# A spectral filter with a gated feed-forward: more block products of seven, maxima over partitions by matmul, and a table of due times

## The chip, the cores and the metric

The kernel runs on one core of a Trainium2 chip. The metric is the device time of one execution in microseconds (us). The core has five engines, each of which works through its own instructions in program order: TensorE (PE), with its weight loads shown apart (PEld), VectorE (DVE), ScalarE (ACT), GpSimd (POOL) and SyncE (SP), which issues nearly all DMAs.

## The reference

x is 2048 rows by 512 columns, F is 1376; everything is f32.

```python
xn = _layernorm(x, axis=-1)
X = rfft2(xn, axes=(-2, -1)) * (w_r + 1j * w_i)
s = irfft2(X, s=(2048, 512), axes=(-2, -1))
gate = xn @ W_gate
gate = gate * (gate > 0)
h = gate * (xn @ W_up)
out = x + s * silu(h @ W_down)
```

## The kernel before, in words

Every product of matrices is made of f16 parts: each operand is split into a high part and a low part (high = round to f16, on ACT mostly; low = value less high, on DVE), and three passes, high x high, high x low, low x high, are added in PSUM (`PASSES`). A first few products of row block 0 use f32 operands, before the split ones are there (`whole` in `product`, L854).

**The feed-forward.** The 2048 rows are four row blocks c of 512 (`NBL` = 4). F is cut into eleven tiles f of 128 columns, the last (f = 10) of 96. For each c and f, `product` (L837) makes gate and up, [128 of F] x [512 rows], with 12 matmuls of 512 columns each; `rectify` (L883) takes the gate's positive part r on ACT, `hidden` (L895) multiplies it with up on DVE and splits the result into h. `down` (L916) adds the eleven tiles into four results dn of 128 rows x 512 columns for each block, and `gate` (L935) makes g = silu(dn) on ACT. The g of blocks 0 to 2 go to DRAM (G_d) and come back later, those of block 3 stay.

Ten of the eleven tiles form five pairs, `PAIRS` = (0,1), (3,4), (5,6), (7,8), (2,9). A pair has 2 x 2 tiles of 12 matmuls of 512 columns, 48 in all. `fast_products` (L944) makes the same 2 x 2 block product with seven block products of eight, from sums and differences of the blocks (D is halved, and the 512 rows are halved): seven times 12 matmuls of 256 columns, into three PSUM tiles sa, sb, sc, which ACT copies or rectifies on their way (sb from sa, sk from sc, sr and sq the positive parts) and DVE adds and multiplies (sc, se, sr). It needs two things ahead of it: `row_sums` (L478) of the row block, four sums sx of normalised rows, split, written to DRAM and brought back transposed as xS; and `weight_sums` (L682) of the pair, which loads the raw weights again (rp), scales them on ACT, makes four sums on DVE, and splits them into wT and into the place of part of up's weights in wgu. So after it the pair can't be made in the plain way.

Before, `PLAINS` says which pairs of which block are fast: in block 3 the pairs 0, 2, 3 and 4; all others are plain.

**The scales.** Weights are scaled by powers of two before they are split. The one for W_down needs the greatest value over all 128 partitions of a column md, the filter's needs that of mw. `greatest` (L728) writes the column to a row in DRAM and reads the row back onto all partitions, then takes the maximum on DVE. The scale scd and with it the split of W_down's rows (wds) wait for this.

**The filter.** The 2-D transform runs in stages of matmuls over eight chunks. Chunk c of x is folded and split (`fold`, `split`), the first stage (L582, tile s) goes to DRAM as A_d (from a tile t); for each of eight chunks q of the other axis, `fft_chunk` (L1026) has the stages y, xx, the filter (tt, pf), z and v, with a split (ACT the high half, DVE the low) between any two, and writes C_d; `last_stage` (L1188) reads ct from C_d, makes s2 on PE, and adds and subtracts halves on DVE and POOL (zz, ae, ye) into sv. `finish` (L1237) multiplies sv by g and adds x: for a chunk whose entry in `ADDS` is 'DMA', SP copies x to the output early and POOL issues an accumulating DMA of the product; else x is loaded into xt, added on DVE and stored by SP.

**What sets the order.** Every piece of work is a `step` (L123) of the class `Plan` with an engine, a cost, what it reads and writes, a due time and, for loads, a lead. `run` (L142) passes due times backwards from each step to those it needs, then fills the engines greedily: each time the step that can begin first, among those of one engine that can begin within 0.06 us the one with the smallest due. The steps are then written out in that order, so that the order on each engine is fixed. Tables at the top of the file (due times, which engine does which sum) are its inputs. All instructions are issued through one helper and so have one line in the profile, L87 (L197 after the change): tiles tell them apart.

## Time and profile before

| what | before |
|---|---|
| runs | 405.9, 404.8, 405.76 us |
| median | 405.76 us |
| profiled execution | 403.82 us |
| its span in the trace | 402.0 us |
| PE busy, matmuls | 394.6 us, 3148 |
| DVE busy | 324.1 us |
| ACT busy | 232.2 us |
| POOL busy | 31.8 us |

The span is from the first to the last thing that the profile records; the profiled execution has 1.82 us around it. In the listings below a row of a group reads: line, engine, operation, tile written <- tiles read (buffer numbers left out), shapes, count, then busy time in us, mean ns of one, and the idle time of the engine before them with what ended it. A row of the timeline begins with its start in us and its duration; what stands in brackets is the engine's idle time before it and what ended that. A row of waits reads: who waited <- for whom, us in total, times, longest. Busy time of a group counts overlapping instructions once.

### The profile page before, as it was taken

How to read it: one execution, taken by the hardware profiler on the slowest of the kernel's cores; microseconds unless marked ns; L12 is line 12 of the kernel's file. 1: busy time of each engine (PE TensorE's matmuls, PEld its weight loads, DVE VectorE, ACT ScalarE, POOL GpSimd, SP SyncE). 2: the span in 40 equal slices, each digit the busy share in tenths (PEclk: the TensorE clock that was granted, in tenths of full speed). 3: DMA queues.
4: the chain of work that ended last, by engine and by line, in shares of the span. 5: the costliest groups of instructions: out<-in, count | busy, mean ns of one | idle time of the engine just before them, and what ended most of it. 6: DMA issues, size and time to landing. Idle time of an engine off the chain costs nothing.

```text
span 402.0 us, 8180 instructions
## 1 busy us (share of the span) xinstructions
PE 394.6 (98%) x3148; PEld 225.4 (56%) x3148; DVE 324.1 (81%) x731; ACT 232.2 (58%) x458; POOL 31.8 (8%) x48
## 2 busy tenths in 40 slices
PE   8999998999999999999999999999999999999996
PEld 6954443544444454554545655556554766888545
DVE  4989997998978989369488589987995665988893
ACT  5999993578579954232563554736464635456311
POOL 0000000000000000014001020010110002404100
PEclk9999999999999999999999999999999999999999
DMA  7963220509599717924047009479445496967452
GB/s 253 398 222 104 91 55 7 157 11 228 180 307 322 247 51 298 230 98 127 31 122 247 2 1 292 142 237 228 104 90 178 139 237 212 197 193 182 110 182 105
DMA packets 53367, 66.50 MB, mean 165 GB/s; under 512 B 20752, under 2 KB 30832, under 8 KB 53328
## 3 DMA queue, kind: packets, MB, share of 16 engines
q1 hardware_dynamic: 52176, 63.89, 53.0%
q0 software_dynamic: 1152, 2.10, 3.4%
q8 instruction: 24, 0.39, 0.4%
q14 instruction: 15, 0.12, 0.1%
HBM read 42.89 MB, written 20.99 MB: 159 GB/s over the span
## 4 chain that ended last, share of the span: by engine, by line
PE 85%; ACT 9%; DMA 2%; DVE 1%; issue 1%; SPq 0%; ACTq 0%
PE gu L87 34%; PE dn L87 27%; PE sb L87 4%; ACT wgu L87 4%; PE s L87 3%; PE z L87 3%; PE sa L87 3%; PE xx L87 3%; PE sc L87 3%; DMA A_d<-t 2%; PE y L87 2%; PE small L87 2%; PE v L87 2%; ACT wds L87 1%; ACT r L87 1%; ACT xf L87 1%
## 5 line engine op out<-in xcount | busy, mean ns | idle before, releaser
L87 PE MATMUL gu<-xT,wgu 128*128 128x512 f16 (+1 forms) x768 | 165.3, 372 | 2.4 <-ACT r L87 1.8
L87 PEld LDWEIGHTS <-wgu 128*128 128x128 f16 x960 | 92.9, 98 | 89.3 <-issue 5.3
L87 PE MATMUL dn<-wds,h 128*128 128x512 f16 (+2 forms) x528 | 115.8, 372 | 0.3 <-ACT g L87 0.3
L87 PEld LDWEIGHTS <-h 128*128 128x128 f16 (+1 forms) x594 | 54.5, 98 | 56.2 <-issue 2.2
L87 ACT ACTIVATE h<-h 128x512 f16<-128x512 f32 (+1 forms) x36 | 22.0, 624 | 29.5 <-DVE h L87 29.5
L87 DVE TENSOR_TENSOR h<-gu,r 128x512 f32<-128x512 f32 (+3 forms) x44 | 27.6, 627 | 11.6 <-PE gu L87 8.6
L87 ACT ACTIVATE r<-gu 128x512 f32<-128x512 f32 (+2 forms) x36 | 20.7, 578 | 21.2 <-PE gu L87 18.2
L87 POOL TENSOR_TENSOR tt<-tt,tt 128x256 f32<-128x256 f32 x8 | 8.6, 1076 | 253.6 <-DVE tt L87 224.1
L87 DVE TENSOR_TENSOR h<-h,h 128x512 f16<-128x512 f32 (+1 forms) x36 | 23.8, 684 | 1.9 <-ACT h L87 1.8
L87 DVE SCALAR_TENSOR_TENSOR tt<-xsp,cw,wt 128x512 f32<-128x512 f32 x32 | 24.5, 819 | 0.0
L87 ACT ACTIVATE g<-dn,cdi 128x512 f32<-128x512 f32 (+1 forms) x16 | 10.8, 672 | 19.0 <-PE dn L87 17.4
L87 PE MATMUL gu<-xT,wgt 128*64 128x256 f16 (+1 forms) x144 | 17.0, 309 | 0.0
L87 DVE TENSOR_TENSOR z<-z,z 128x1024 f16<-128x1024 f32 x8 | 9.8, 1222 | 7.8 <-ACT z L87 7.7
L87 DVE TENSOR_TENSOR a<-y,a 128x1024 f16<-128x1024 f32 x8 | 9.7, 1223 | 7.9 <-ACT a L87 7.9
L87 PEld LDWEIGHTS <-wT 128*128 128x128 f16 x144 | 13.9, 98 | 3.1 <-issue 0.4
L87 DVE SCALAR_TENSOR_TENSOR wgu<-raw,p,wgu 128x512 f16<-128x512 f32 x20 | 14.5, 746 | 1.0 <-ACT wgu L87 1.0
L87 DVE TENSOR_TENSOR t<-v,t 128x1024 f16<-128x1024 f32 x8 | 9.7, 1220 | 6.8 <-ACT t L87 6.8
L87 ACT ACTIVATE z<-z 128x1024 f16<-128x1024 f32 x8 | 8.2, 1023 | 11.2 <-PE z L87 11.2
L87 DVE TENSOR_TENSOR t<-s,t 128x896 f16<-128x896 f32 (+1 forms) x16 | 10.6, 686 | 4.7 <-ACT t L87 4.7
L87 ACT ACTIVATE a<-y 128x1024 f16<-128x1024 f32 x8 | 8.1, 1024 | 9.5 <-PE y L87 9.5
L87 PEld LDWEIGHTS <-wgt 128*64 128x64 f16 (+1 forms) x144 | 9.7, 106 | 6.1 <-issue 0.8
L87 ACT ACTIVATE wgu<-raw 128x512 f16<-128x512 f32 x20 | 12.3, 620 | 0.0
(191 smaller groups left out, 596.8 us busy)
## 6 DMA issues: line engine op xcount, KB each, us to landing
A_d<-t SPq DMA_DIRECT2D x16, 256.0 KB, 4.1
rw<-in_wl SPq DMA_DIRECT2D x8, 512.0 KB, 5.9
wt<-in_wl SPq DMA_DIRECT2D x8, 512.0 KB, 7.0
at<-A_d SPq DMA_DIRECT2D x8, 512.0 KB, 5.2
C_d<-t SPq DMA_DIRECT2D x16, 256.0 KB, 3.4
ct<-C_d SPq DMA_DIRECT2D x16, 256.0 KB, 5.7
x<-in_x SPq DMA_DIRECT2D x7, 512.0 KB, 5.9
G_d<-g SPq DMA_DIRECT2D x12, 256.0 KB, 3.5
```

The source lines that it names most:

```text
L87: return lambda *args, **kw: self.tc.keep_in_program_order(f(*args, **kw))
```

## The change

1. `PLAINS` gives way to `fast(c, n)`, with `FASTS` = 2, 1, 2, 2, 2 blocks counted from the last. Block 3 then has all five pairs fast, block 2 the pairs 0, 2, 3 and 4: five more fast pairs in all. This adds `row_sums` for block 2 (with two more transposing DMAs) and `weight_sums` for pair 1, and the due times of the weight sums become a table (`TDUE`).
2. `weight_sums` keeps its raw weights in two tiles, one for gate and one for up, where it had one.
3. `greatest` multiplies a unit matrix by the column on DVE, brings it to all partitions with one f32 matmul by ones, and takes the maximum on DVE from PSUM. The two DMAs and the row in DRAM go.
4. After the backward pass of due times, `run` sets each step's due from a table `DUES`, and each lead from a table `WAITS`. With other numbers in the tables at the top (engines of some sums in `SUM2` and `DIFF2`, `ADDS` of chunk 5 now 'DMA', due times) this gives another order on every engine.

The counts: PE has 182 more matmuls (five times 84 less 48, and two), DVE 30 more rows in its list of instructions, ACT 20 more activations, POOL two more DMAs, SP two more transposes.

```diff
-STATS, ADDS, COPIES = ['DVE', 'DVE', 'ACT', 'DVE', 'ACT', 'ACT', 'ACT', 'ACT'], ['DMA', 'DMA', 'DVE', 'DMA', 'DMA', 'DVE', 'DVE', 'DVE'], [105.83, 259.66, 138.19, 267.03, 599.36, 405.66, 358.32, 606.44]
+STATS, ADDS, COPIES = ['DVE', 'DVE', 'ACT', 'DVE', 'ACT', 'ACT', 'ACT', 'ACT'], ['DMA', 'DMA', 'DVE', 'DMA', 'DMA', 'DMA', 'DVE', 'DVE'], [105.83, 202.31, 0.24, 342.73, 748.16, 416.58, 501.03, 895.66]
...
-TPREP, TSTEP, XLEAD = 205.365, 26.484, 13.97
+TDUE, XLEAD = [158, 242, 202, 219, 235], 17.37
...
-PLAINS = ['plain', 'plain', 'plain', 'plain', 'plain', 'plain', 'plain', 'plain', 'plain', 'plain', 'plain', 'plain', 'plain', 'plain', 'plain', 'fast', 'plain', 'fast', 'fast', 'fast']
+FASTS = ['2', '1', '2', '2', '2']
+DUES = (
+    61.11, 143.08, 138.41, 136.86, 1e+09, 1e+09, 1e+09, 1e+09, 1e+09, 1e+09, 1e+09, 1e+09, 1e+09, 1e+09, 1e+09, 1e+09, 1e+09, 1e+09, 1e+09, 1e+09,
...
+def fast(c, n):
+    return c >= NBL - int(FASTS[n])
...
+        for s, due in zip(steps, DUES):
+            s.due = due
+        for s, lead in zip([s for s in steps if s.lead is not None], WAITS):
+            s.lead = lead
...
-        tile_of(raw, "xg", [P, 2, 4, 2 * P], F32)
         for i, src in enumerate((wg, wu)):
+            tile_of(f"{raw}_{i}", "k4", [P, 4, 2 * P], F32)
...
-        row = dram.tile([1, P], F32, name=f"row_{name}")
-        tile_of(f"rows_{name}", "k2", [P, P], F32)
-        rows = lambda: T[f"rows_{name}"]
-        top = cpool.tile([P, 1], F32, name=f"max_{name}")
-        step("SP", .6, lambda: SP.dma_start(row.rearrange("a p -> p a"), col), reads=reads, writes=[f"row_{name}"], due=due, kb=8, lag=3.)
-        step("SP", .6, lambda: SP.dma_start(rows(), row.broadcast_to([P, P])), reads=[f"row_{name}"], writes=[f"rows_{name}"], kb=64, lag=5.2)
-        step("DVE", .22, lambda: DVE.tensor_reduce(top, rows(), axis=AX.X, op=ALU.max), reads=[f"rows_{name}"], writes=[f"all_{name}"], due=due + 10)
+        wide, top = f"wide_{name}", cpool.tile([P, 1], F32, name=f"max_{name}")
+        tile_of(wide, "k2", [P, P], F32)
+        tile_of(f"rows_{name}", "F", [P, P], F32)
+        step("DVE", .25, lambda: DVE.tensor_scalar(T[wide], unit, col, None, op0=ALU.mult), reads=reads, writes=[wide], port=True, due=due)
+        step("PE", .26, lambda: matmul(T[f"rows_{name}"], ones, T[wide], start=True, stop=True), reads=[wide], writes=[f"rows_{name}"], due=due + 2)
+        step("DVE", .3, lambda: DVE.tensor_reduce(top, T[f"rows_{name}"], axis=AX.X, op=ALU.max), reads=[f"rows_{name}"], writes=[f"all_{name}"], due=due + 4)
...
-        if c and f < TAIL and PLAINS[5 * c + n] == "fast":
+        if f < TAIL and fast(c, n):
...
-            if PLAINS[5 * c + n] == "plain":
+            if not fast(c, n):
...
-            if PLAINS[5 * c + n] == "fast" and PLAINS[5 * c - 5 + n] == "plain":
-                weight_sums(n, TPREP + n * TSTEP)
+            if c == NBL - int(FASTS[n]):
+                weight_sums(n, TDUE[n])
```

The order of the instructions is shown at two places. The first is SP's list from the start of the program, with the loads of x and of the raw weights of gate (in_wg) and up (in_wu). Before:

```order
1 L87 DMA x_143<-in_x 128x512 x2
2 L87 DMA raw_0_150<-in_wg 128x512
3 L87 DMA raw_1_155<-in_wu 128x512
4 L87 DMA x_170<-in_x 128x1024 [waits Pool_49]
5 L87 DMA raw_0_174<-in_wg 128x512 [waits Pool_49]
6 L87 DMA raw_1_187<-in_wu 128x512
7 L87 DMA raw_0_196<-in_wg 128x512
8 L87 DMA raw_1_203<-in_wu 128x512 [waits DMAHW0_49]
9 L87 DMA raw_0_212<-in_wg 128x1024 [waits DMAHW1_49]
10 L87 DMA raw_1_224<-in_wu 128x1024 [waits DMAHW2_49]
11 L87 DMA x_229<-in_x 128x1024 [waits DMAHW3_49]
12 L87 DMA x_240<-in_x 128x1024 [waits DMAHW4_49]
```

And after the change:

```order
1 L197 DMA x_141<-in_x 128x512 x2
2 L197 DMA raw_0_148<-in_wg 128x512
3 L197 DMA raw_1_153<-in_wu 128x512
4 L197 DMA x_157<-in_x 128x1024
5 L197 DMA x_161<-in_x 128x1024
6 L197 DMA x_177<-in_x 128x1024 [waits Pool_49]
7 L197 DMA raw_1_189<-in_wu 128x512
8 L197 DMA raw_0_182<-in_wg 128x512 [waits DMAHW0_49,Pool_49]
9 L197 DMA raw_1_208<-in_wu 128x1024 [waits DMAHW1_49]
10 L197 DMA raw_1_217<-in_wu 128x512 [waits DMAHW2_49]
11 L197 DMA raw_0_225<-in_wg 128x512 [waits DMAHW3_49]
12 L197 DMA raw_0_240<-in_wg 128x1024 [waits DMAHW4_49]
```

The x that waits for POOL is chunk 1, which with chunk 0 (row 1) makes row block 0. Chunks 2 and 3, rows 11 and 12 before, now stand ahead of it, as rows 4 and 5, and the weights behind it come in another order.

The second place is the end of DVE's list. sv_5252, sv_5353 and sv_5365 are the filter's results of chunks 7, 5 and 6; g_0 to g_3 are the gates dn3_0 to dn3_3 of row block 3, g_2l and g_3l those of block 2 that come back from DRAM. Before (sv_5044 and sv_5055 are chunks 6 and 7):

```order
674 L87 TENSOR_TENSOR sv_5044<-sv_5044,g_0_5006 128x512 [waits DVE_49,Activation_49]
675 L87 TENSOR_TENSOR sv_5044<-sv_5044,g_1_5072 128x512 [waits Activation_49]
676 L87 TENSOR_TENSOR xt_0_5051<-xt_0_5051,sv_5044 128x512 [waits DMAHW4_49,DVE_49]
677 L87 TENSOR_TENSOR sv_5055<-sv_5055,g_2_5123 128x512 [waits Activation_49]
678 L87 TENSOR_TENSOR xt_1_5065<-xt_1_5065,sv_5044 128x512 [waits DMAHW5_49,DVE_49]
679 L87 TENSOR_TENSOR xt_0_5086<-xt_0_5086,sv_5055 128x512 [waits DMAHW6_49,DVE_49]
680 L87 TENSOR_TENSOR sv_5055<-sv_5055,g_3_5191 128x256 [waits Activation_49]
681 L87 TENSOR_TENSOR xt_1_5092<-xt_1_5092,sv_5055 128x256 [waits DMAHW7_49,DVE_49]
682 L87 TENSOR_TENSOR sv_5055<-sv_5055,g_3_5191 128x128 [waits Activation_49]
```

After:

```order
702 L197 TENSOR_TENSOR sv_5252<-sv_5252,g_2_5389 128x512 [waits Activation_49]
703 L197 TENSOR_TENSOR sv_5353<-ye_5271 128x2x255
704 L197 TENSOR_TENSOR xt_0_5263<-xt_0_5263,sv_5252 128x512 [waits DMAHW5_49,DVE_49]
705 L197 TENSOR_TENSOR sv_5365<-sv_5365,g_1_5403 128x512 [waits Activation_49]
706 L197 TENSOR_TENSOR sv_5353<-sv_5353,g_2l 128x512 [waits DMAHW0_49,DVE_49]
707 L197 TENSOR_TENSOR sv_5252<-sv_5252,g_3_5439 128x128 [waits Activation_49]
708 L197 TENSOR_TENSOR sv_5353<-sv_5353,g_3l 128x512 [waits DMAHW1_49]
709 L197 TENSOR_TENSOR xt_1_5285<-xt_1_5285,sv_5252 128x128 [waits DMAHW7_49,DMAHW2_49,DVE_49]
710 L197 TENSOR_TENSOR xt_1_5371<-xt_1_5371,sv_5365 128x512 [waits DMAHW2_49]
...
715 L197 TENSOR_TENSOR xt_0_5408<-xt_0_5408,sv_5365 128x512 [waits DMAHW3_49]
```

Chunk 5 was finished before block 3's last gates, and its x was added on DVE. Now its second half (703) and its products by block 2's gates (706, 708) stand behind a product by g_2 of block 3 (702), POOL issues its two accumulating DMAs behind 706 and 708, and the list ends with the addition of x to chunk 6 (715).

More of the change, by code (lines that the diff above doesn't have):

```diff
@@ L706, in weight_sums @@
         minus((1, 0), (1, 1), (1, 0), U + [t1], t3)
-        minus((1, 1), (1, 1), (0, 0), U + [t1, t3], t2)
+        minus((1, 1), (1, 1), (0, 0), G + U + [t1, t3], t2)
         minus((0, 1), (0, 1), (1, 1), G + [t2], t4)
-        for to, of, needs, k in ((slice(0, 2), lambda: T[raw][:, 0].rearrange("p (t k) f -> p t k f", t=2), [t1, t4, t2], 0),
-                                 (slice(2, 3), lambda: B(1, 1).unsqueeze(1), [t2, t4], 2)):
+        for to, of, needs, k in ((slice(0, 2), lambda: T[f"{raw}_0"].rearrange("p (t k) f -> p t k f", t=2), [*G, t1, t4, t2], 0),
+                                 (slice(2, 3), lambda: B(1, 1).unsqueeze(1), [*U, t2, t4], 2)):
             m = 512 * (to.stop - to.start)
@@ L718, in weight_sums @@
             of = lambda j=j: B(1, 0)[:, :, j * P:j * P + P]
-            step("ACT", act(256), lambda to=to, of=of: ACT.activation(to(0), of(), AF.Copy), reads=[t3], writes=[("wgu", f, 0, 1)], due=due + 2)
-            step("DVE", dve(256), lambda to=to, of=of: DVE.tensor_sub(to(1), of(), to(0)), reads=[t3, ("wgu", f, 0, 1)], writes=[("wgu", f, 1, 1)], port=True, due=due + 4)
+            step("ACT", act(256), lambda to=to, of=of: ACT.activation(to(0), of(), AF.Copy), reads=[*U, t3], writes=[("wgu", f, 0, 1)], due=due + 2)
+            step("DVE", dve(256), lambda to=to, of=of: DVE.tensor_sub(to(1), of(), to(0)), reads=[*U, t3, ("wgu", f, 0, 1)], writes=[("wgu", f, 1, 1)], port=True, due=due + 4)
     def weights(f, i):
@@ L1293 @@
                 turn(k, LOWS[k])
-            if k > 1 and k % 2 and any("fast" in PLAINS[5 * (k // 2) + n] for n in range(len(PAIRS))):
+            if k > 1 and k % 2 and any(fast(k // 2, n) for n in range(len(PAIRS))):
                 row_sums(k // 2)
```

49 lines of the change are left out of this document (27 added, 22 removed), and 99 rows, old and new, of tables (DUES, WAITS).

## The prediction, on record before the run

> **What bounds the kernel now.** I read the page's busy times first, then TensorE's (PE's) waits, then the busy time of each engine in stretches of the span.
>
> ```profile
> span 402.0 us, 8180 instructions
> PE 394.6 (98%) x3148; PEld 225.4 (56%) x3148; DVE 324.1 (81%) x731; ACT 232.2 (58%) x458; POOL 31.8 (8%) x48
> PEclk9999999999999999999999999999999999999999
> GB/s 253 398 222 104 91 55 7 157 11 228 180 307 322 247 51 298 230 98 127 31 122 247 2 1 292 142 237 228 104 90 178 139 237 212 197 193 182 110 182 105
> ...
> PE gu L87 <- ACT r L87: 1.8, 1, 1.8
> PE small L87 <- DVE md L87: 1.1, 1, 1.1
> PE gu L87 <- DVE h L87: 0.6, 1, 0.6
> PE dn L87 <- ACT g L87: 0.3, 1, 0.3
> ```
>
> PE is busy 98% of the span at an undiminished clock, and its whole list of waits is 3.8 us, of which 1.1 us is the start. Removing PE columns therefore shows in the time, unless another engine becomes late. In the stretches (start:end, length, then busy time of PE, PEld, DVE, ACT, POOL) the same is seen:
>
> ```profile
> 97.00:176.00 79.00, 79.00 (x592) 38.75 (x591) 62.79 (x162) 47.75 (x90) 0.00 (x0) 1.00 0.71 229
> 176.00:283.00 107.00, 107.00 (x920) 57.87 (x919) 85.51 (x155) 54.55 (x84) 12.40 (x12) 1.00 0.48 140
> 283.00:362.00 79.00, 79.00 (x743) 51.64 (x742) 60.73 (x107) 39.71 (x77) 12.26 (x19) 1.00 0.65 167
> 362.00:402.00 40.00, 36.51 (x316) 24.36 (x313) 30.69 (x67) 12.30 (x34) 6.10 (x10) 1.00 0.53 145
> ```
>
> From 97 to 362 us PE stands still for nothing; VectorE (DVE) is busy 209.0 of those 265 us. DVE is the second bound: 56 us of room there, 21.5 us of it in the 107 us from 176 to 283.
>
> **Term 1, the products: -5.8 us.** A plain pair of gate and up is 48 matmuls of 512 columns. A fast pair is seven block products of 12 matmuls of 256 columns, 84 in all. The first row below is a run of 60 of the former, the next two are block products of block 3 that stand one behind the other; the last is the mean of one weight load.
>
> ```profile
> 23.95 13.11 PE L87 MATMUL gu<-xT,wgu 128*128 128x512 f16 x60
> ...
> 312.30 1.48 PE L87 MATMUL sa<-xT,wgu 128*128 128x256 f16 x12
> 313.62 1.47 PE L87 MATMUL sc<-xS,wgu 128*128 128x256 f16 x12
> ...
> L87 PE MATMUL gu<-xT,wgu 128*128 128x512 f16 x720 | 159.5, 379 | 1.8 <-ACT r L87 1.8
> L87 PE MATMUL gu<-xTf,raw 128*128 128x128 f32 x64 | 8.0, 278 | 0.1
> L87 PEld LDWEIGHTS <-wgu 128*128 128x128 f16 x960 | 92.9, 98 | 89.3 <-issue 5.3
> ```
>
> The 60 take 13.11 less the 0.38 of one alone over 59 steps, 0.216 us each, so a plain pair is 48 x 0.216 = 10.36 us. Twelve of the latter take 313.62 - 312.30 = 1.32 us, 0.110 each, so a fast pair is 7 x 1.32 = 9.2 us. The gain is 1.16 us a pair, and five pairs turn fast (four in block 2, pair 1 in block 3): -5.8 us. The down products keep their count and shape.
>
> A rule of the Trainium skill speaks against this term. Its page "TensorE: Matmul & The Clock Gate", section "Back-to-back issue gap", says that in a stream where each matmul has its own weight load the spacing is set by both, about 131 ns at 512 columns and 81 ns at 128; an estimate between them for 256 columns, about 98 ns, would make a fast pair 8.2 us against 6.3 us, a loss of 1.9 us a pair. The rows above give 216 and 110 ns, in step with the columns, so they do not agree, and the sum goes by the rows.
>
> **Term 2, maxima by matmul: +0.25 us on PE.** Two f32 matmuls of 128 columns are added; 64 such take 8.0 us, so 0.125 each. DVE's multiplication and maximum take the place of one maximum; below half a microsecond on DVE, in a stretch before 97 us and near 140 us. What this removes is in term 4.
>
> **Term 3, the head: +2.4 us (0 to 4.1).** In the new order two whole blocks of x (0.5 MB each) are issued ahead of the second half-block's x, on the same queue.
>
> ```profile
> 3.81 0.33 SPq L87 DMA_DIRECT2D x<-in_x  x1
> ...
> 17.61 1.58 PE L87 MATMUL gu<-xT,wgu 128*128 128x256 f16 x13
> ```
>
> This x, issued at 3.81, leads through statistics, normalisation and transposition to the first split products at 17.61. 1.05 MB more ahead of it take 2.6 us at the 398 GB/s of the second slice, 4.1 us at the 253 of the first, and nothing if PE's earlier work hides it. That work, f32 products on unsplit weights, is short of covering it, since its weights now come in another order too: I take 2.4, just under the faster rate.
>
> **Term 4, early waits: -2.7 us (0 to -2.7).** The way of the down weights' maximum through DRAM, before:
>
> ```profile
> 54.73 0.54 SPq L87 DMA_DIRECT2D row_md<-md  x1
> ...
> 64.14 0.32 SPq L87 DMA_DIRECT2D rows_md<-row_md  x1
> ...
> 65.00 0.63 ACT L87 ACTIVATE x<-xf 128x512 f16<-128x512 f32 x1 [5.03 <-DMA A_d<-t]
> ...
> 66.16 2.75 PE L87 MATMUL gu<-xT,wgu 128*128 128x512 f16 x12 [1.81 <-ACT r L87]
> ```
>
> The 128 writes of 4 bytes and the reading back occupy the queue from 54.73 past 64.14, while the memory moves 55 and then 7 GB/s. The transfers A_d<-t that stand beside them land late, ScalarE (ACT) waits 5.03 us for one, its r comes late, and PE waits 1.81 us. With the route through PE no DMA stands there. The 0.6 and 0.3 us of PE's list lie in the same setup (before 97 us), where a later start of PE gives ACT and DVE the time. I take all 2.7; none if ACT and DVE are as late as PE.
>
> **Term 5, more work on DVE and ACT: +0.9 us (0 to 15).** Mean durations on DVE:
>
> ```profile
> L87 DVE TENSOR_TENSOR h<-h,h 128x512 f16<-128x512 f32 x32 | 21.2, 684 | 1.9 <-ACT h L87 1.8
> ...
> L87 DVE TENSOR_TENSOR rp<-rp 128x512 f32<-128x512 f32 x16 | 11.0, 687 | 1.4 <-ACT rp L87 1.2
> ...
> L87 DVE TENSOR_TENSOR wT<-rp,wT 128x1024 f16<-128x1024 f32 x4 | 4.9, 1216 | 0.0
> ...
> L87 DVE TENSOR_TENSOR se<-sb,sk 128x512 f32<-128x512 f32 x4 | 2.8, 692 | 0.9 <-PE sb L87 0.7
> ...
> L87 DVE TENSOR_TENSOR wgu<-rp,wgu 128x256 f16<-128x256 f32 x8 | 3.3, 418 | 0.0
> ```
>
> A fast pair has six DVE operations of 512 where a plain one has four: 2 x 0.69 = 1.4 us, 7.0 for five. The sums of pair 1's weights are five of 512, one of 1024 and two of 256: 5 x 0.687 + 1.22 + 0.84 = 5.5 us. The row sums of block 2 are four of 512 and two of 1024, 5.2 us. Together 17.7 us. They go into the 56 us of room, so on the average nothing need wait. But in 176 to 283 us come block 2's four pairs (5.6), the sums of pair 1 (5.5) and, by the new due times, those of two further pairs in exchange for one (net 5.5): 16.6 us against 21.5 us of room. Every block product of a fast pair waits for a copy or sum by ACT or DVE, as every stage of the transform does. I take 0.9 us, near the nothing that PE waited in before's two stretches at 77 and 80%; the other end is 15 us, most of the added work with no room used.
>
> **Term 6, the tail: +2.8 us (1.5 to 4.9).** The end of before, then DMA rows (KB, median us from issue to landing: three earlier and the last two accumulating DMAs of GpSimd (POOL), and the last stores), then two means:
>
> ```profile
> 397.34 1.17 PE L87 MATMUL dn_3bb<-wds,h 128*128 128x128 f16 x18
> 398.55 0.37 ACT L87 ACTIVATE g<-dn_3bb,cdi 128x128 f32<-128x128 f32 x1 [0.64 <-PE dn_3bb L87]
> 398.95 0.29 DVE L87 TENSOR_TENSOR sv<-sv,g 128x128 f32<-128x128 f32 x1 [0.39 <-ACT g L87]
> 399.28 0.29 DVE L87 TENSOR_TENSOR xt<-xt,sv 128x128 f32<-128x128 f32 x1
> ...
> out<-sv POOLq DMA_DIRECT2D x3, 256.0 KB, 7.9
> ...
> out<-sv POOLq DMA_DIRECT2D x2, 256.0 KB, 5.8
> ...
> out<-xt SPq DMA_DIRECT2D x5, 256.0 KB, 2.5
> out<-xt SPq DMA_DIRECT2D x1, 128.0 KB, 1.7
> ...
> L87 ACT ACTIVATE g<-dn,cdi 128x512 f32<-128x512 f32 x15 | 10.3, 685 | 14.6 <-PE dn L87 13.0 <-DVE ye L87 1.6
> ...
> L87 DVE TENSOR_TENSOR sv<-sv,g 128x512 f32<-128x512 f32 x3 | 2.0, 683 | 0.3 <-ACT g L87 0.3
> ```
>
> Before, PE ends at 398.51 and the span 3.5 us later; of this about 0.7 us lies behind the last landing (402.0 - 399.57 - 1.7). In the new order DVE's row 702 needs the gate of dn3_2, whose last matmul is followed by 3 of 512, 33 of 256 and 18 of 128 columns: 0.65 + 3.6 + 1.0 = 5.3 us of PE (18 small ones take 1.17 at the end of before). Rows 702 to 708, six operations of 512 and one of 128, stand behind that gate, and the last finishes chunk 5 for POOL's accumulating DMA. The gate takes 0.69, they 6 x 0.69 + 0.29 = 4.4, so POOL issues 0.2 us before PE ends. It lands 5.8 us later; with the closing 0.7 the span ends 6.3 us behind PE, 2.8 more than before. The direct path (rows 709 to 715, another 3.1 us, a store of 2.5, the closing) gives 6.1, or 5.0 if operations that stand back to back overlap by a tenth of a microsecond; that is the low end. The high end is an accumulation of 7.9 us.
>
> The Trainium skill's "DMA: Bandwidth & Descriptors", section "Anatomy of one DMA — SWDGE (gpsimd) path", gives 2.0 us plus the bytes at 436 GB/s, an estimate of 2.6 us here. The row of 5.8 disagrees; by the page the direct path would end last, and the sum would be 0.2 to 1.3 us lower.
>
> **The sum.** -5.8 + 0.25 + 2.4 - 2.7 + 0.9 + 2.8 = -2.15 us. Against the profiled execution, 403.82 (span 402.0 and 1.82 around it), this is 401.7. The median of the runs, 405.76, lies 1.94 higher; I carry the change over: 403.6.
>
> **The rivals.**
>
> - *The whole gain shows* (DVE's room suffices, the direct path ends): term 5 is 0 and term 6 is 1.5, sum -4.35, 401.4 us. For it: 265 us without a wait before. Against it: POOL's DMA at 5.8 us.
> - *The early waits stay*: x arrives later for ACT and DVE too, so that they trail PE as before. Term 4 is 0, sum +0.55, 406.3 us, no change that can be measured. For it: in PE's list of waits ACT and DVE are what PE waited for in the setup. Against: the DMA that caused the largest wait is gone.
> - *Slower, by DVE in 176 to 283 us*: the room of 21.5 us is mostly time in which DVE has nothing ready, since it waits for PE or ACT in the middle of a chain. If three quarters of it cannot be filled, 16.6 us of work meet 5.4 of room; half of the excess can still move past 283, and PE waits about 6 us. Sum -2.15 + 5.1 = +2.95, 408.7 us. It decides from 3.0 us of waits in that stretch (0.9 + 2.15). For it: the order is fixed when the program is made, and a late operation cannot be overtaken. Against: before at 80% had no wait at all.
> - *The change doesn't save columns' time*: weight loads of 98 ns each would have to stand between the matmuls. A fast pair has 84 loads against 48, 3.5 us more, 17.6 for five beside the sum without it, 421.2 us. The spacing of 110 ns with a load of 98 ns inside it excludes it nearly. The rule of the Trainium skill's page "TensorE: Matmul & The Clock Gate" that is weighed at term 1 goes in this direction; its estimate in place of term 1 would give 418.9 us.
>
> **Chances.** The forecast 0.42, the whole gain 0.20, early waits that stay 0.19, DVE late 0.17, loads 0.02. The range reaches from 1.2 us below the whole gain, 400.2, to 407.8, where DVE's rival begins to weigh; what lies beyond is about 2 in 10. A difference of 0.3% (1.2 us) is about what a measurement of this kernel can tell from none. Faster by more: 0.60 (nearly all of the first two cases); within: 0.20; slower: 0.20.
>
> **What would show it.** Right: PE's busy time 5 to 6 us less, no wait of PE at 66 us, the first split product at about 20 us, PE's waits from 97 to 362 under 2 us, and POOL's out<-sv as the last landing 5 to 7 us behind PE's end. Wrong: waits of PE for DVE's or ACT's se, sr, sb or for the transform's low halves of more than 3 us in all, an accumulation that takes 9 us or more, or a first split product beyond 22 us.

## The result, and the profile after

The changed kernel takes 409.4 us (median of 6 executions, 408.26 to 410.49) against 404.52 for the kernel before (6, 403.54 to 405.9): ratio 1.0119, interval 1.0092 to 1.0145, slower by about 4.9 us. The forecast was 403.6 with a range to 407.8. Over all measurements the executions of the kernel before fall, but for a few, into two groups, about 404 us at a granted clock of 0.998 to 1.0 and about 406 us at 0.996, so a ratio given below can differ from that of the medians (e14: 0.9947 and 0.9969). The profiled execution of the changed kernel took 408.49 us, span 406.7; all rows of "after" are from it. From its page and from the list of PE's waits:

```profile
span 406.7 us, 8600 instructions
PE 391.2 (96%) x3332; PEld 242.9 (60%) x3332; DVE 339.0 (83%) x755; ACT 245.4 (60%) x478; POOL 30.8 (8%) x50
...
PE gu L197 <- ACT xTf L197: 1.7, 1, 1.7
PE dn L197 <- ACT g L197: 1.4, 1, 1.4
PE small L197 <- DVE md L197: 1.1, 1, 1.1
PE rows_mw L197 <- DVE wide_mw L197: 1.0, 1, 1.0
PE sc L197 <- DVE sr L197: 0.9, 1, 0.9
```

The wait of 1.8 us at 66 us is gone, and four of about 1 to 1.7 us have come (the whole list makes 7.1 us with three small ones; before it made 3.8). By stretches, as before (start:end, length, busy time of PE, PEld, DVE, ACT, POOL):

```profile
97.00:176.00 79.00, 78.01 (x480) 36.59 (x479) 66.80 (x155) 51.40 (x97) 0.00 (x0) 1.00 0.72 224
176.00:283.00 107.00, 106.06 (x1116) 72.79 (x1114) 95.77 (x181) 64.87 (x101) 6.31 (x8) 1.00 0.62 168
283.00:362.00 79.00, 79.00 (x873) 59.16 (x871) 58.00 (x101) 39.57 (x73) 13.58 (x22) 1.00 0.58 144
```

From 176 to 283 us DVE went from 85.5 to 95.8 of 107 us, and PE stood for only 0.94 us there. The end of after: first the chain of work that ended last (start, duration, engine, tile), cut to its turning points, then PE's last row in the timeline, then SP's last stores (ns of one issue; time of the first and the last issue; landing), then the DMA rows of the last 13 us.

```profile
382.24 11.02 PE dn L197 x51
...
393.42 0.70 ACT g L197
...
400.02 0.60 DVE xt L197
...
396.71 1.80 PE L197 MATMUL dn<-wds,h 128*128 128x256 f16 x15
...
L197 SPq DMA_DIRECT2D out<-xt x6: 332/344/531, 396.1 to 400.8; - x6
...
DMA to landing us min/median/max: 1.6/3.4/4.9
...
out<-sv POOLq DMA_DIRECT2D x2, 256.0 KB, 5.1
out<-xt SPq DMA_DIRECT2D x2, 64.0 KB, 3.3
out<-xt SPq DMA_DIRECT2D x1, 128.0 KB, 4.7
```

PE ends at 396.71 + 1.80 = 398.51, where it ended before (398.51 too): the columns' gain is eaten on the way. The chain leaves PE at 393.26 and runs on ACT and DVE for seven microseconds, to 400.62; the last store is issued at 400.8 and lands 4.7 us later, and the span ends 8.2 us behind PE, 3.5 before. (The 3.3 us of the two 64 KB stores is the middle of two unlike ones: 1.6 for the one issued at 398.3, 4.9 for the one at 399.7.) So PE lost on the way as much as the columns gained, and the 4.7 us by which the span grew all lie behind PE's last matmul.

For what PE lost on the way I took the start of each matmul less that of the one before, less the median of that spacing for its shape in before's trace (0.216 us at 512 columns, 0.109 at 256), and added what is over by stretches of the span:

| stretch, us | over, before | over, after | difference |
|---|---|---|---|
| 0 to 25 | 3.46 | 5.71 | +2.25 |
| 25 to 50 | -0.10 | -0.18 | -0.08 |
| 50 to 100 | 5.06 | 3.27 | -1.79 |
| 100 to the end of PE | 16.40 | 21.65 | +5.25 |
| columns at the median spacing | 372.41 | 366.74 | -5.67 |
| span behind the end of PE | 3.5 | 8.2 | +4.7 |

The differences add up to the 4.7 us of span. Of the 5.25, three stalls make 3.86: 1.16 at 172.7 us, 1.10 at 222.0 and 1.60 at 363.8; the other 1.39 lie in no gap over 0.3 us. In the timeline of after (start, duration, engine; in brackets the idle time before, and what ended it):

```profile
173.62 0.29 DVE L197 TENSOR_SCALAR wide_mw<-unit,mw 128x128 f32<-128x128 f32 x1
174.05 0.46 PE L197 MATMUL rows_mw<-wide_mw,ones 128*128 128x128 f32 x2 [0.99 <-DVE wide_mw L197]
...
221.50 0.42 DVE L197 TENSOR_TENSOR pf<-tt,tt 128x256 f32<-128x256 f32 x1 [2.35 <-DMA C_d<-t]
222.51 0.69 DVE L197 TENSOR_TENSOR sr<-sb,sr 128x512 f32<-128x512 f32 x1
223.25 0.93 PE L197 MATMUL sc<-xS,wgu 128*128 128x256 f16 x7 [0.94 <-DVE sr L197]
...
364.68 0.21 ACT L197 ACTIVATE ye<-zz 128x2 f32<-128x2 f32 x1 [1.94 <-DMA out<-sv]
364.79 0.67 ACT L197 ACTIVATE g<-dn,cdi 128x512 f32<-128x512 f32 x1
365.51 1.24 PE L197 MATMUL dn<-wds,h 128*128 128x512 f16 x5 [1.44 <-ACT g L197]
```

The first is a wait that the change made itself: the matmul of the new route for mw stands in PE's list at a place that PE reaches before its operand is there. In the second, DVE stands 2.35 us until a DMA to C_d is done, and sr, which PE needs, is queued behind. In the third, ACT stands 1.94 us at a copy of two columns until an accumulating DMA of POOL's is done, and the gate g, which PE's next dn waits for, is queued behind.

### The profile page after: what moved, and what is told of

The parts are those of the page before. It is cut to its first block, busy times and chain, and to the rows that moved or that the text cites. A ratio compares the mean times of both kernels' runs of the same rounds, so it can differ in the third digit from the quotient of the medians.

```text
span 406.7 us, 8600 instructions
## 1 busy us (share of the span) xinstructions
PE 391.2 (96%) x3332; PEld 242.9 (60%) x3332; DVE 339.0 (83%) x755; ACT 245.4 (60%) x478; POOL 30.8 (8%) x50
## 4 chain that ended last, share of the span: by engine, by line
PE 59%; DVE 17%; DMA 12%; ACT 5%; issue 2%; SPq 2%; POOL 0%; DVEq 0%; ACTq 0%
PE dn L197 17%; PE gu L197 13%; PE sb L197 7%; PE sc L197 5%; PE sa L197 5%; DVE h L197 3%; DMA A_d<-t 3%; PE z L197 3%; PE xx L197 3%; DVE xs L197 2%; SPq L197 2%; PE y L197 2%; DVE t L197 2%; DMA x<-in_x 2%; DMA out<-sv 2%
## 5 line engine op out<-in xcount | busy, mean ns | idle before, releaser
L197 PE MATMUL gu<-xT,wgu 128*128 128x512 f16 (+1 forms) x528 | 111.9, 369 | 0.4 <-DVE xT L197 0.4
L197 PEld LDWEIGHTS <-wT 128*128 128x128 f16 x324 | 31.3, 98 | 6.0 <-issue 0.5
L197 POOL TENSOR_TENSOR pf<-tt,tt 128x256 f32<-128x256 f32 x12 | 10.1, 846 | 264.2 <-ACT xsp L197 184.3
L197 PE MATMUL sa<-xT,wgu 128*128 128x256 f16 x216 | 26.6, 273 | 0.0
L197 PE MATMUL sb<-xS,wT 128*128 128x256 f16 x216 | 26.6, 273 | 0.0
L197 DVE TENSOR_TENSOR h<-gu,r 128x512 f32<-128x512 f32 (+3 forms) x34 | 20.7, 608 | 1.8 <-ACT r L197 1.0
L197 ACT ACTIVATE r<-gu 128x512 f32<-128x512 f32 (+2 forms) x26 | 14.9, 574 | 10.8 <-PE gu L197 10.7
L197 PE MATMUL sc<-xS,wgu 128*128 128x256 f16 x108 | 13.3, 273 | 0.9 <-DVE sr L197 0.9
L197 POOL TENSOR_TENSOR ae<-zz 128x126 f32<-128x126 f32 (+1 forms) x18 | 10.7, 722 | 40.7 <-issue 37.6
L197 ACT ACTIVATE rp<-rp,csc 128x512 f32<-128x512 f32 x20 | 13.4, 714 | 0.0
L197 PE MATMUL sc<-xT,wT 128*128 128x256 f16 x108 | 13.3, 273 | 0.0
```

What stands on the lines that cost most here:

```text
L197: return lambda *args, **kw: self.tc.keep_in_program_order(f(*args, **kw))
```

## The experiments

In several of them the order of the instructions is written out as a list of steps in place of the planner's, so that single steps can be moved and nothing else changes. Where an edit moves steps of such a list, it is given below in words and shortened:

```diff
-        order.sort(key=lambda k: k[0])
+        order = [(0., steps[i]) for i in ORDER]
```

**e1, chunk 5 stored.** The one change of `ADDS` undone, with due times for the two additions of x that it brings back.

```diff
-STATS, ADDS, COPIES = [...], ['DMA', 'DMA', 'DVE', 'DMA', 'DMA', 'DMA', 'DVE', 'DVE'], [...]
+STATS, ADDS, COPIES = [...], ['DMA', 'DMA', 'DVE', 'DMA', 'DMA', 'DVE', 'DVE', 'DVE'], [...]
```

> The changed kernel with chunk 5 finished as before the change (x added on DVE, stored by SP) in place of POOL's accumulating DMA; the order on PE is that of the changed kernel. Theory (contention at the end: two accumulating DMAs share the DMA engines with the last stores, and the last store takes 4.5 us in place of 2): PE still ends at about 398.5 us, DVE ends 1.2 us later than 400.6, the span ends at 404 to 404.5, 2 to 2.5 us earlier than 406.7. Rival (DVE is what ends late, and the stores are slow whatever POOL does): two more DVE operations, the span ends 1 us later, at 407.5 to 408.

Ratio to before 1.0055 (1.0021 to 1.0088), 406.59 us: 2.6 us of the loss, by the ratios, go with the accumulation of chunk 5. Its profiled execution was the slowest of ten (410.12 us) and shows less of this: the span ends 7.2 us behind PE, 3.5 of them until DVE's end, and PE's wait for wide_mw was 2.11 us, to which the last section returns.

**e2, e3, e4, the parts planned anew.** e2 is after without the assignment of due times from `DUES` (the leads stay). e3 is before with five more pairs fast, e4 before with the new `greatest`; both leave the order to before's planner.

```diff
-        for s, due in zip(steps, DUES):
-            s.due = due
...
+PLAINS = ['plain'] * 10 + ['fast', 'plain', 'fast', 'fast', 'fast'] + ['fast'] * 5
...
-        step("SP", .6, lambda: SP.dma_start(row.rearrange("a p -> p a"), col), reads=reads, writes=[f"row_{name}"], due=due, kb=8, lag=3.)
+        step("PE", .26, lambda: matmul(T[f"rows_{name}"], ones, T[wide], start=True, stop=True), reads=[wide], writes=[f"rows_{name}"], due=due + 2)
```

> The changed kernel without the table of due times (the dues come from the backward pass; the leads stay from their table), so that the last stages of chunks 5 and 6 stand 37 us of PE's work ahead of its end in place of 18. Theory (the order that the table gives makes the last stages late, and DVE ends late for that): the last DVE operation at most 1 us behind PE's end, span 401 to 403, some 4 us less than with the table. Rival (the added 17.7 us of DVE work are what costs, in any order): PE waits move to other places, span 406 or more.

> The kernel before with the five more fast pairs alone (with the row sums of block 2 and the weight sums of pair 1), maxima through DRAM and dues as before. Theory (columns are worth their time where the order leaves DVE room): 6.0 us of PE work less, 2 to 3 us of it given back in waits between 170 and 330 us, ratio to before 0.990 to 0.993. Rival (DVE's 17.7 us more make PE wait in any order): ratio 1.000 to 1.015.

> The kernel before with the maxima by matmul alone. Theory (PE's wait of 1.81 us at 66 us came from the writes of 4 bytes on the queue): that wait is gone, first rows otherwise as before, 1.5 to 2 us less, ratio 0.995 to 0.997. Rival (the new matmul makes PE, which works in order, wait for DVE's product of unit and column where the DMA made nobody wait): a wait of about 1 us each at md and mw, ratio 0.999 to 1.003.

Ratios 1.0723 (1.0663 to 1.0783), 1.1213 (1.1153 to 1.1273) and 1.0386 (1.0323 to 1.0449), e3 and e4 far slower than either case that was expected. One wait of PE, which ends at 376.5 us, long after the maxima, carries most of e4's loss:

```profile
PE sb L87 <- DVE se L87: 11.8, 1, 11.8
```

In these three the order of all steps changed together with the part, so they do not give the parts' own cost. From here on the order was held.

**e5 and e8, the head's loads.** The loads of the blocks x2 and x3 put behind that of x1, in after's order (e5); e8 is e5, e6 and e7 together.

```diff
 SP x0
 SP raw0 (wg, wu)
-SP x2
-SP x3
 SP x1
+SP x2
+SP x3
```

> The changed kernel in its own order, written out as a list, with one thing moved: the loads of chunks 2 and 3 of x stand behind the load of chunk 1. Theory (the later x1 sets PE's first split product and the delay stays to the end): first split product at 18 us in place of 20, 2 us less in all, ratio to before 1.005 to 1.008 where the changed kernel has 1.012. Rival (ACT and DVE bound the setup, the delay is taken up before 100 us): the time of the changed kernel, 1.010 to 1.014.

> The moves of the head, of the three waits and of the tail together. Theory (the gain of 5.8 us of columns is there and was lost at these places): 2 + 3.3 + 3 us less than the changed kernel, span 398 to 399, ratio 0.989 to 0.993, faster than before. Rival (DVE's 17.7 us more of work are the cause, so waits move elsewhere): ratio 1.000 or more.

e5 is worse than after: 1.0167 (1.0135 to 1.0199). Two rows of it:

```profile
12.44 0.69 DVE L263 BATCH_NORM_STATS2 st<-x 128x6 f32<-128x512 f32 x1 [3.11 <-DMA x<-in_x]
...
12.38 3.60 PE L263 MATMUL gu<-xTf,raw 128*128 128x128 f32 x16 [3.83 <-ACT xTf L263]
```

The loads moved, but the statistics of x3 and x2 still stood ahead of those of x1 on DVE and ACT, and now waited for the later loads: PE's wait grew to 3.83 us. e8 (1.0052, 1.0027 to 1.0077) carries the same head and is slower than e9, its like without it. Here the queue could not be reordered without the lists that wait for it.

**e6, the three stalls.** In after's order, three moves.

```diff
-PE:  rows_mw, four products of dn
+PE:  four products of dn, rows_mw (its maximum and the scale on DVE later too)
-DVE: pf (filter), tt, sr2_0
+DVE: sr2_0, pf (filter), tt
-ACT: ye0 (copy), g2_2
+ACT: g2_2, ye0 (copy)
```

> The changed kernel in its own order, with three places moved: the matmul of mw's maximum four down products later on PE (and its maximum and scale later on DVE); DVE's sr of pair 0 of block 2 ahead of the filter sum that waits for a DMA; ACT's gate of block 2 ahead of a copy that waits for an accumulating DMA. Theory (each wait of PE costs its length to the end): waits of 1.0, 0.9 and 1.4 us gone, PE ends at 395 in place of 398.5, span 403 to 404, ratio 1.003 to 1.006. Rival (DVE is full, so what is moved ahead makes something else as late): PE's waits sum to 6 us or more as before, ratio 1.010 to 1.014.

404.72 us, ratio 1.0003 (0.9983 to 1.0023): by the ratios the three moves give back the 1.2% that was lost. That is 4.7 us, more than the stalls' 3.86 but within the intervals. The profiled execution, the slowest of twelve (406.51 us), shows a part: PE ends at 396.0 instead of 398.5, with a new wait of 1.60 us for a gate g at 177.9.

**e7, the tail.** In after's order, the last 17 instructions of DVE in another sequence: the products of chunk 5 (sv5, for POOL) earlier, the narrow pieces of the last result last.

```diff
-DVE: sv6*g, sv5, sv7*g, sv5, xt7_0, sv6*g, sv5*g, ..., sv5*g, ..., xt7_1, xt6_0
+DVE: sv5, sv5, sv6*g, sv5*g, sv5*g, sv7*g, xt7_0, sv6*g, xt6_1, xt6_0, ..., xt7_1
```

> The changed kernel in its own order, with the last 17 operations of DVE reordered: chunk 5 ahead of the products by block 3's last gates, the parts by the last gate at the very end, and what stores them behind each. Theory (late issue of the accumulating DMAs and of a whole block's store makes the tail): PE ends at 398.5, DVE at 400.3, last landing 2 us later in place of 5, span 403 to 404, ratio 1.003 to 1.006. Rival (the stores are slow since DMA is busy with the accumulation whatever the order): span 406 to 407.

406.65 us, ratio 1.0045 (1.002 to 1.0069): 0.7% less than after. PE ends at 398.07, the span at 404.94, so 6.9 us behind it instead of 8.2.

**e9, e6 and e7 together.**

> The order of the changed kernel with both moves together: the three waits moved as in e6_three_waits and the last 17 VectorE instructions moved as in e7_tail_order; nothing else. Theory: the two losses are separate, one in front of TensorE's last matmul (2.5 us taken back by e6) and one behind it (8.2 us between that matmul and the end of the span, of which e7 left 6.9), so the savings add: TensorE ends near 395.8, the span near 401.5, ratio 0.991 to 0.996. Rival: VectorE's work behind 375 us is what ends last, whatever TensorE does; then the end stays where e6 had it, span 404.6, ratio 1.000.

403.31 us, ratio 0.9978 (0.9955 to 1.0). PE ends at 393.84 and the span at 401.0 (7.2 us). By the ratios this is 1.4% less than after, of the 1.9% that the two take off singly: between the two cases that were expected. DVE has no room at the end (same columns as the stretches above):

```profile
375.00:395.00 20.00, 18.84 (x159) 11.27 (x151) 19.79 (x44) 6.88 (x19) 6.63 (x8) 1.00 0.94 221
```

**e10, the maxima alone, order held.** Before's order, with the three steps of each maximum replaced and placed where I thought that nobody need wait for them (the code is e4's).

> The kernel before with the two greatest values found by matmul and nothing else, and with all other instructions left in the order of before (its order written out instead of planned again, which e4_only_maxima did not do). The widened row, its matmul and the reduction are put so that nobody waits for them. Theory, Term 4 and Term 2 of the prediction: the wait of 1.81 us at 66 us goes and nothing of its size takes its place, two small matmuls add 0.25 us: 1.6 us less, ratio 0.994 to 0.997. Rival: the wait was only a cover for the next one (the down weights' scaling waits for VectorE's queue), then under 0.5 us are gained, ratio 0.999 to 1.001.

405.09 us, ratio 1.0006 (0.9983 to 1.0029): no gain, as the rival said. Where before waited at 66 us, this kernel waits a little later, for the next things that ACT and DVE owe:

```profile
65.08 2.75 PE L150 MATMUL gu<-xT,wgu 128*128 128x512 f16 x12 [0.18 <-ACT r L150]
...
72.11 0.59 PE L150 MATMUL dn<-wds,h 128*128 128x512 f16 x2 [0.59 <-DVE wds L150]
73.87 1.50 PE L150 MATMUL gu<-xT,wgt 128*64 128x256 f16 x24 [1.16 <-ACT r L150]
```

1.8 us became 0.18 + 0.59 + 1.16 = 1.93. But the new steps did make others wait. The first row is ACT in before, the next three are ACT and DVE in e10:

```profile
54.08 0.60 ACT L87 ACTIVATE r<-gu 128x512 f32<-128x512 f32 x1 [0.16 <-PE gu L87]
...
58.15 0.60 ACT L150 ACTIVATE r<-gu 128x512 f32<-128x512 f32 x1 [3.90 <-DVE xs L150]
...
61.09 0.28 DVE L150 TENSOR_REDUCE max_md<-rows_md 128x1 f32<-128x128 f32 x1
...
69.98 0.23 DVE L150 TENSOR_SCALAR scd<-rho,pd 128x11 f32<-128x11 f32 x1
```

ACT no longer waits 5.03 us for A_d<-t at 60 us, but 3.90 us at 54 us, until DVE has done with xs<-ee; r, ee and the new wide_md are tiles of one pool (k2), so I take it that wide_md holds the buffer that r had before, which no run shows. And the maximum is there at 61.4, while scd, which needs it, keeps its old place in DVE's list. So e10 shows that the new route gains nothing at these places in before's order, and not what it gains in an order made for it.

**e11, plain last writes.** After, with POOL's two writes of chunk 5 plain; the addition of x for that chunk is left out.

```diff
-POOL.dma_start(to, T[sn][:, i, :], accum_op=ALU.add)
+POOL.dma_start(to, T[sn][:, i, :], **({} if c == 5 else {"accum_op": ALU.add}))
```

> The changed kernel, with its last two accumulating writes (POOL's out<-sv of chunk 5) as plain writes of the same bytes at the same places; the addition of x for that chunk is left out. Theory: the accumulating DMAs share the 16 engines with the last stores and hold each packet up, 5.1 us from issue to landing; as plain writes they land in 2 to 3.5 us, the last store too, and the span ends 1.5 to 2.5 us sooner than the changed kernel's: ratio 1.004 to 1.009. Rival: the stores at the end are late for their number of bytes (1.3 MB in 7 us) and for VectorE, not for the accumulation: the same time as the changed kernel, ratio 1.010 to 1.014.

405.45 us, ratio 1.0036 (1.0015 to 1.0058), 0.8% less than after. Its DMA rows of the end:

```profile
out<-sv POOLq DMA_DIRECT2D x2, 256.0 KB, 2.8
out<-xt SPq DMA_DIRECT2D x2, 64.0 KB, 2.3
out<-xt SPq DMA_DIRECT2D x1, 128.0 KB, 2.4
```

The same bytes from the same places of the lists land in 2.8 us instead of 5.1, and the stores beside them in 2.3 and 2.4 instead of 3.3 and 4.7. The span ends 6.0 us behind PE (397.46, 403.4) instead of 8.2.

**e12, e9 with chunk 5 stored** (the edit of e1; the rest of the order is e9's).

> e9 with chunk 5 added on VectorE and stored from SP instead of accumulated by POOL (as in e1_chunk5_stored): two more additions of 0.68 us on VectorE behind 375 us, two loads of x, no accumulating DMA among the last stores. Theory: VectorE is full to the end and the additions cost 1.2 us there, the stores then land within 3 us of VectorE's end instead of 5: 0.5 to 1.5 us less than e9, ratio 0.988 to 0.994. Rival: the additions put VectorE's end further behind TensorE's, and the loads of x come late: 1 us or more above e9.

404.04 us, ratio 0.9987 (0.996 to 1.0014), no better than e9 and short of the gain that was expected. DVE pays for two more additions, and the first of them waits for its x:

```profile
391.40 0.69 DVE L270 TENSOR_TENSOR xt<-xt,sv 128x512 f32<-128x512 f32 x1 [1.26 <-DMA xt<-in_x]
```

DVE ends at 398.53, 3.9 us behind PE (1.8 in e9); the last store then lands 1.7 us behind DVE's end (4.1 in e9).

**e13, the head as before.** After, with the order of x0's halves, x1, the raw weights, x2 and x3 as before, and the statistics of x2 and x3 moved behind those of x1 on ACT and DVE. **e14** is e9 with this head, **e15** is e14 with e11's plain writes (the addition of x for chunk 5 is left out).

```diff
-SP: x0 (second half), x0 (first half), raw0, x2, x3, x1, raw2, raw1, ...
+SP: x0 (first half), x0 (second half), raw0, x1, raw1, raw2, raw3, x2, x3, ...
-DVE, ACT: statistics of x3, x2, then x1
+DVE, ACT: statistics of x1, then (after 19 us) x3, x2
```

> The changed kernel with its head set back to the order of before, and nothing else: the half of x's first block that VectorE and POOL read is loaded first, the second half-block's x next, the blocks x2 and x3 behind the first four pairs of weights, and (unlike e5_head_order) their statistics on ScalarE and VectorE behind those of the second half-block. Theory, Term 3: the head's 2.25 us come from the order of loads and of the statistics that wait for them; the first split product starts at 17.3 to 18.3 us instead of 19.4 to 20.0, and the kernel is 1.5 to 2.2 us shorter than the changed one: ratio 1.006 to 1.009. Rival, what e5 and e8 seemed to say: the order of after is the best there is for its order of weights, and the head stays at 19.4 or later: ratio 1.011 or more.

> e9_waits_and_tail with the head of e13_head_as_before. Theory: what kept e9 only 0.2 per cent below the kernel before is the head; with it set back the column savings of Term 1 come through but for the tail: 1.5 to 2 us less than e9, ratio 0.992 to 0.995, TensorE's last matmul at 391.5 to 392.5. Rival: with TensorE earlier, the waits for VectorE grow by as much and the end stays: ratio 0.997 to 0.999.

> e14 with the last two accumulating writes (chunk 5) as plain writes, as in e11_plain_last_writes; the addition of x for that chunk is left out. It tells what of Term 6 is the accumulation and what is VectorE's late end. Theory: the accumulation holds the last stores up by the 2 to 3 us that e11 gained, also here: 2 to 3 us less than e14, ratio 0.985 to 0.989, and the last landing within 3 us of VectorE's last instruction. Rival: with the tail reordered the accumulating DMAs are issued 3 us earlier and no longer meet the last stores: under 0.7 us less than e14.

e13: 408.33 us, ratio 1.0089 (1.0063 to 1.0115); e14: 403.2, 0.9947 (0.9927 to 0.9967); e15: 401.57, 0.9917 (0.9886 to 0.9949). e14 has the whole function and is faster than the kernel before (by 0.5% in the ratio, 0.3% in the medians) and than after. But the head's part in it is not resolved: e13 lies 0.3% under after and e14 0.3% under e9, and both intervals overlap. The timeline of e13:

```profile
18.19 0.27 PE L263 MATMUL gu<-xT,wgu 128*128 128x256 f16 x1
18.84 1.36 PE L263 MATMUL gu<-xT,wgu 128*128 128x256 f16 x11 [0.38 <-DVE xT L263]
...
22.55 1.26 PE L263 MATMUL gu<-xT,wgu 128*128 128x256 f16 x10 [0.45 <-DVE wgu L263]
24.09 0.60 PE L263 MATMUL gu<-xT,wgu 128*128 128x512 f16 x2 [0.27 <-ACT wgu L263]
```

The first split product starts 1.9 us earlier than after's (20.05), and PE then waits for the next weights, which ACT and DVE still split in after's order. Over its median spacing e13's PE stands 5.28 us up to 25 us, after's 5.71, before's 3.46. Traces of e11, e7, e6 and e9, which have after's head unchanged, give 5.30, 5.22, 5.10 and 4.80, so the 0.4 us is within what one head varies by. PE does end 2.3 us earlier in e13 than in after, but mostly behind 100 us, where its trace has no wait for wide_mw and 0.95 us for the gate g. e15 against e14 takes 0.3% more off, less than was expected, with intervals that overlap; the span ends 5.0 us behind PE instead of 6.6.

## Why the prediction was wrong, point by point

**What bounds** (PE's columns, DVE second) was right, and so was that the gain shows only if nothing else becomes late.

**Term 1 (-5.8)** was right: 5.67 us with Term 2's matmuls in it, some 6.1 without them. In after a block product follows the other after 1.31 us, 0.109 us for each matmul:

```profile
227.15 1.47 PE L197 MATMUL sb<-xS,wT 128*128 128x256 f16 x12
228.46 1.47 PE L197 MATMUL sa<-xT,wgu 128*128 128x256 f16 x12
```

PE's busy time fell by 3.4 us and not by the 5 to 6 that I gave as a sign, since a matmul of 512 columns counts for 379 ns in it and the next begins after 216, so that short stalls hide in busy time. The rule of the Trainium skill that was weighed here (131 and 81 ns; page "TensorE: Matmul & The Clock Gate", section "Back-to-back issue gap") disagrees with these rows as well. **Term 2 (+0.25)** is too small to be told apart in the time. The profile has two records for each f32 matmul of this kind (184 matmuls more than before, where the account of the change above counts 182), and four at 0.112 us are 0.45 us. Its matmuls hold a term that I left out, too: the one for mw can wait, and did, for 1.0 us.

**Term 3 (+2.4)** had the right size, 2.25 us, and the first split product started where I said, at 20.05:

```profile
20.05 0.27 PE L197 MATMUL gu<-xT,wgu 128*128 128x256 f16 x1
```

That the size fits is in part luck: the other four traces of the same head give 1.3 to 1.8 us (4.80 to 5.30 less before's 3.46). The cause that I named, the x loads, is not borne out: with these set back (e13) the product came 1.9 us earlier, and what is left of that by 25 us, 0.4 us, cannot be told from none. The head's order of weights on ACT and DVE is what is left; no run set it back alone, so this stays open.

**Term 4 (-2.7)** had the right sign and most of the size (1.79 us from 50 to 100 us); its cause stays open. In e10 the DMAs went and nothing was gained, but there the new steps made ACT wait 3.90 us and scd came no earlier than before; in after the first wds begins at 62.3 us, in before at 69.1. Whether PE's wait went away in after by the new route, by the new order or because PE comes 2.25 us later, no run tells.

**Term 5 (+0.9) is the step that failed first.** I priced an engine's queue by its load: DVE had room, so little would wait. The load itself was read well enough (DVE's busy time grew by 14.9 us, 17.7 were priced). The measured cost behind 100 us is 5.25 us, 3.86 of it in three stalls, and only one of them is in the stretch whose room I had counted (16.6 against 21.5 us). None came from lack of room: in each, an in-order engine (PE, DVE, ACT) stood at an instruction whose operand or buffer came late (wide_mw, the DMA to C_d, the accumulating DMA), while work that could have gone on stood behind it. e6 only changed these places in the order, with the same work on DVE and ACT, and the 1.2% came back. In the measure of the table above, PE stands 18.12 us behind 100 us in e9 and 18.39 and 18.14 in e14 and e15, which have these moves, against 21.65, 21.62 and 21.12 in after, e7 and e11, which do not (e6, with its new wait for g: 19.67); in e9's list PE has no wait there. What stays over before's 16.40, about 1.7 us, stands in no gap over 0.3 us, and its cause is open. My sign of being right, under 2 us of waits from 97 to 362 us, even held (0.99 and 0.94): the third stall came just behind that stretch. I could have seen it: in before, the same copy into ye waited for the same accumulating DMA, with no PE behind it (3.7 us in all for the eight copies; 1.9 after).

```profile
L87 ACT ACTIVATE ye<-zz 128x2 f32<-128x2 f32 x8 | 1.6, 200 | 3.7 <-DMA out<-sv 3.7
```

**Term 6 (+2.8) was mis-sized**; it measured +4.7. Which path ends was close between two, and the sum took the wrong one: POOL's DMAs took 5.1 us to land (4.2 and 6.1), the second at 404.5, and SP's last store landed at 405.4. On the direct path I priced the last store at 2.5 us, from rows where no accumulating DMA ran beside it. With the 4.7 us that it took, the 6.1 us of that path become 8.3; measured are 8.2, though that fits so well because two errors cancel: DVE ended 2.1 us behind PE and not 2.9, and 1.3 us passed from the last landing to the span's end and not 0.7. e11 and e15 show the main cause: with plain writes in place of the accumulation the end behind PE shrinks by 2.2 us (8.2 to 6.0) and by 1.6 (6.6 to 5.0). Of the other 2.5 us, 1.0 is DVE, which ends 2.1 us behind PE where it ended 1.1 behind before; the rest no run takes apart. DVE works 24.07 of the 25 us from 375 to 400 us in after, 20.47 in before:

```profile
375.00:400.00 25.00, 23.52 (x209) 14.22 (x206) 24.07 (x56) 7.39 (x22) 6.63 (x8) 1.00 0.78 197
...
375.00:400.00 25.00, 23.51 (x175) 14.12 (x172) 20.47 (x46) 5.35 (x13) 1.77 (x2) 1.00 0.50 146
```

(the first row is after, the second before). e7 takes 1.3 us off the end by order alone.

**The rivals.** The kernel became slower, but not by the rival that said so: it put about 6 us of waits for DVE into 176 to 283 us, and there were 0.94. The rival by which the early waits stay did not come true in after (1.79 us went), nor that of the weight loads (0.109 us a matmul). The whole gain does not show in any order tried here: e14, the best that has the whole function, takes 3.4 us off PE's end and leaves 6.6 us behind it, 3.5 before, and its median lies 1.2 us under the kernel before. **The sum**: with the measured sizes, -5.67 + 2.25 - 1.87 + 5.25 + 4.7 = 4.66 us of span (the third number is 25 to 100 us); the forecast of -2.15 missed by 4.35 us in Term 5, 1.9 in Term 6, and 0.8 in Term 4. As a time the forecast missed by 5.8 us only, since it stood on a median of 405.76 from three executions of before, where six gave 404.52.

## What to carry to other kernels

Where each engine keeps its own order, the price of added work need not be its share of an engine's idle time (here 0.9 us became 5.25): go through the instructions that already wait for a DMA in the trace, and ask what stands behind them in the new order. Price the last stores by rows in which the same DMAs run beside them; here an accumulating DMA near the end cost the stores as well (4.7 us against 2.4). A frozen order with single moves separates causes that planning anew mixes up, as long as the steps put in make nobody wait, which e10's did.

## What the runs showed of the hardware that was not expected

**After one wait of 2.1 us the granted clock was half, after one of 2.6 us it was not.** In e1 PE waits 2.11 us at 172.6, and the next nine matmuls take 3.78 us; nine of the same, a little later, take 2.12. The second view gives the granted clock (the first number behind POOL's): 0.50 in 175 to 178 us, 1.00 later.

```profile
174.75 0.52 PE L204 MATMUL rows_mw<-wide_mw,ones 128*128 128x128 f32 x2 [2.11 <-DVE wide_mw L204]
175.06 3.78 PE L204 MATMUL dn<-wds,h 128*128 128x512 f16 x9
...
179.58 2.12 PE L204 MATMUL dn<-wds,h 128*128 128x512 f16 x9
...
175.00:178.00 3.00, 3.00 (x9) 1.10 (x9) 2.76 (x13) 0.72 (x2) 0.00 (x0) 0.50 0.89 232
180.00:184.00 4.00, 4.00 (x70) 2.24 (x69) 2.96 (x3) 3.14 (x5) 0.00 (x0) 1.00 0.49 106
```

So a wait of 2.1 us cost 1.7 us more than itself. e5's wait of 3.83 us did the same (its 16 f32 matmuls took 3.60 us, 2.05 in after). Waits of 1.8 us in before, of 1.7 in after and of 1.6 in e6 left the clock at 1.00. The Trainium skill, page "TensorE: Matmul & The Clock Gate", section "What's actually happening", has the array fall to half its clock after an idle window of about 3.4 us; here 2.11 us was enough. The length of a wait does not decide alone, however: PE's longer waits of 2.36 us in e2 and of 2.56 us in e3 left the clock at 1.00.

```profile
214.01 1.50 PE L197 MATMUL z<-cD,p 128*128 128x128 f16 x24 [2.36 <-DVE a L197]
...
297.14 0.39 PE L87 MATMUL sc<-xS,wgu 128*128 128x256 f16 x2 [2.56 <-ACT wgu L87]
```

In the clock records of all seventeen traces the clock changes only at multiples of 3.41 us from the first record: e1's half clock lasts 3.41 us, those of e2 while PE works 3.41, 6.83, 3.41 and 10.24. I cut each trace into windows of 3.41 us, counted from its first record of the clock. Of the windows at full clock, every one in which PE had no matmul running for 2.11 us or more is followed by half clock, and every one with 1.86 us or less by full clock, but one (e2 at 52.5 us: 1.20 us, with a few matmuls of 4 columns in it). e1's wait lies in one window, those of e2 and e3 across two. So where a wait falls counts as well as its length; no run moved a wait to test this. The mean clock of whole executions fits: in after's profiled one it is 0.994, all that is missing lying behind PE's end, and in four of the six it is 0.990 or 0.991, about one more window at half clock (half of 3.41 us is 0.004 of the span); that such a window fell into them is not shown.

**The accumulating DMAs took nearly twice as long here as plain ones of their size, and the stores beside them too**: 5.1 against 2.8 us for POOL's 256 KB, and 4.7 against 2.4 us for a 128 KB store (after and e11). After moves POOL's bytes in packets of 2048 bytes, e11 in packets of 4096; how much of the difference is the addition and how much the packets, no run tells. The 2.6 us that the prediction worked out from the Trainium skill's page "DMA: Bandwidth & Descriptors", section "Anatomy of one DMA — SWDGE (gpsimd) path", agree with the plain write's 2.8 and not with the accumulation.
